# Cross-covariance attention and multiplicative FFN on one core: the head reordered, with k's squares moved off TensorE

## The chip, the core and the metric

One NeuronCore of a Trainium2 chip runs the whole kernel. The metric is device time in microseconds (us) of one launch. The engines are TensorE (PE, its weight loads PEld), VectorE (DVE), ScalarE (ACT), GpSimd (POOL) and SyncE (SP). SP, ACT and POOL also issue DMAs.

## What is computed

```python
# q, k, v: (4, 5824, 256) float32; tau = 1; B = 4, N = 5824, C = 256
qn = q / (norm(q, axis=1) + 1e-6)          # norms over the 5824 tokens, one for each channel
kn = k / (norm(k, axis=1) + 1e-6)
a  = softmax(kn.transpose(0, 2, 1) @ qn / tau)      # 256 x 256 for each batch
x  = (v @ a).reshape(23296, 256)
out = ((x @ w1) * (x @ w2)) @ w3 @ w_out            # w1, w2: 256 x 1024, w3: 1024 x 1024, w_out: 1024 x 256
```

## The kernel before

Everything is bf16 in SBUF and float32 in PSUM. v @ a @ w1 is taken as v @ (a @ w1): for each batch the 256 x 256 softmax is folded into w1 and w2, which gives `Wf`, 256 x 2 x 1024. Likewise w3 @ w_out becomes one matrix `W_sb`, 1024 x 256. So the main loop has, for each batch b, 12 chunks c of 512 tokens (the last of 192) and 8 columns j of 128: one **slot** is `emit_ab` (L621), with two matmuls for `a` and two for `b` at L627, a cast of `a` to bf16 on ScalarE (L633) and the product `abh` on VectorE (L644). Some slots later `abh` is multiplied by `W_sb` (`emit_half` L675 for the first chunks, `seven_products` L540 with POOL sums after those) and stored from SP. Batch 0 has 96 slots.

**The head**, before slot 0. q and k of batch 0 arrive in six pieces each (128 partitions x 8 rows x 256; the last has 5 rows and 64 left-over tokens), loaded and cast by DMAs that POOL issues (`load_piece`, `load_part`, L120; left-overs L117). The first half of piece 0 comes uncast through SP and ACT (`raw`, L745). TensorE works through the pieces in order: `squares` (L236) puts the 128 x 128 products of k with itself and of q with itself into PSUM, whose diagonals are the squared norms; `products` (L248) adds to `G`, the unnormalised scores. `busy` (L224) issues matmuls on zeros. After the last pieces come, all through `soft_units(0)`:

- `k_first` (L259): k's diagonal, on VectorE; `k_row` (L311): a float32 matmul with ones spreads it over all partitions; `k_step` (L319): Ln, Exp, Ln, Exp on ScalarE give 1/norm, `kr`.
- `q_first` (L328): q's diagonal; `scaled_first`: `scale` (L350) is G times `kr` for one half, `q_norm` (L339 to L342) Ln, Exp, add, reciprocal; then `exps` (L355) for two halves.
- `first_folds`: row sums (L375), the first 256 columns of the folds (`quarter_mm`, L422), their scaling (L431 ScalarE, L433 VectorE) into `Wf`. The next 256 columns and the second 512 (`second_quarter`, `fold`, L398) come in between the first slots.

**The order.** `make_agenda` lists for each batch what is emitted when, by a `clock` that counts the costs of what TensorE was given. For batch 0: three transposes of v on TensorE (L143, copies L145 on ScalarE or L147 on VectorE), the transposes of w3 and of v by DMA on SP (L757, L166), eight `w_unit`s (L837) that make `W_sb`, and the loads of the next batch's q and k, called (qk, 1, piece), and of v. Each load stands on POOL's queue behind `gate` (L615), a 1 x 1 copy from the newest `abh`; (qk, 1, 0) and (qk, 1, 2) stand behind a `hold` (L619) besides, a copy from `vT`, so that POOL's queue stops until SP's transpose of v piece 2 and of v piece 3 has landed.

**Scores of the next batch** run inside batch b's slots. `score_units` (L180) gives four units for each pair of rows, 92 in all: two with a square on ScalarE (L197) and two matmuls into G (L200), two with an add on VectorE (L212). In batch 0 they run from slot 36 to slot 78; `share` gives 32 of them (`EARLY`) to the slots ahead of slot 46 and the others evenly to the rest. A piece holds 16 units.

**The end.** `emit_out` (L687) with the last 192 columns of batch 3: `oleft` is copied by VectorE (L718) and stored for batches 2 and 3 by two DMAs of SP (L721); the last rows are copied by ScalarE (L723) and stored by a DMA of ACT (L725).

Of the kernel before, what the change touches and what calls it, by code (L numbers as in the profile page):

```python
# [25 lines left out]
def kernel(  # L26
# [198 lines left out]

    S = {}

    def squares(nm, pi, slots, end=False):

        if nm not in S:  # L230
            S[nm] = psum.tile([P, CT, P], F32, name=f"sq{nm}_0", **bank("out"))
        t = pieces[nm, 0, pi]
        for i in slots:
            for ct in range(CT):
                cs = slice(ct * P, (ct + 1) * P)
                nc.tensor.matmul(  # L236
                    S[nm][:, ct, :], lhsT=t[:, i, cs], rhs=t[:, i, cs],
                    start=(pi == 0 and i == 0 and ct == 0),
                    stop=(end and i == slots[-1] and ct == CT - 1), skip_group_check=True,
                )  # L240
# [13 lines left out]
    def soft_units(n):  # L254
        st = {}

        def k_first():
            d = work.tile([P, CT, P], F32, tag="sq", name="dk", bufs=2)
            nc.vector.tensor_mul(d, S["k"], ident.unsqueeze(1).to_broadcast([P, CT, P]))  # L259
            st["ksq"] = d.rearrange("p c t -> p (c t)")  # L260

        def scaled_first():
            scale(0)
            q_norm(st["ss"])
            scale(1)
            exps(0)
            exps(1)
# [40 lines left out]
        def k_row():  # L308

            m = psum.tile([P, 512], F32, name=f"row_{n}", **bank("ab"))  # L310
            nc.tensor.matmul(m[:, :C], lhsT=ones_pp, rhs=st["ksq"], start=True, stop=True)  # L311
            st["row"] = m[:, :C]
            st["kr"] = work.tile([P, C], F32, tag="kr", name=f"kr_{n}", bufs=1)
            for i in range(4):
                k_step(i)
# [99 lines left out]
        def quarter_mm(lo, c1, c2):  # L415

            if c2 == 0:
                tag = "ab" if lo == 0 else "out"
                st[lo, c1] = psum.tile([P, 2, 256], F32, name=f"quarter_{lo}_{c1}", **bank(tag))
            m = st[lo, c1]  # L420
            for w in range(2):
                nc.tensor.matmul(  # L422
                    m[:, w, :], lhsT=st["e"][:, c2, c1 * P : (c1 + 1) * P], rhs=w12[:, c2, w, lo : lo + 256],
                    start=(c2 == 0 and w == 0), stop=(c2 == CT - 1 and w == 1), skip_group_check=True,
                )
            if c2 == CT - 1:
                for o in (0, P) if lo == 0 else (slice(0, 256),):
                    cols = slice(o, o + P) if lo == 0 else o
                    dst, src = Wf[n][:, c1, :, lo : lo + 256][:, :, cols], m[:, :, cols]
                    if c1 == 0:  # L430
                        nc.scalar.activation(out=dst, in_=src, func=AF.Copy, scale=st["rs"][:, c1 : c1 + 1])  # L431
                    else:
                        nc.vector.tensor_scalar_mul(dst, src, st["rs"][:, c1 : c1 + 1])  # L433

        def first_folds():
            sum_mm(0)
            for c1 in range(CT):
                quarter_mm(0, c1, 0)
            sum_mm(1)
            for c1 in range(CT):  # L440
                quarter_mm(0, c1, 1)

        def second_quarter():
            for c1 in range(CT):
                for c2 in range(CT):
                    quarter_mm(256, c1, c2)

        if n == 0:
            return [k_first, k_row, q_first, scaled_first, first_folds, second_quarter, sum_start] + [lambda i=i: fold(i) for i in range(4, 8)]
# [28 lines left out]
    out_tiles = {}  # L478
    lefts = {}
# [207 lines left out]
    def emit_out(b, c, j, ab, only=None):  # L687
# [24 lines left out]
        if j == FT - 1:  # L712
            o = work.tile([P, 4, D], F32, tag="o_sb", name=f"osb_{b}_{c}", bufs=3)
            rows = out[b * N : b * N + NT * P, :].rearrange("(p i) c -> p i c", i=NT)
            if small:
                if b % 2 == 1 and only != 0:
                    o2 = work.tile([P, D], F32, tag="kr", name=f"oleft_{b}", bufs=1)
                    nc.vector.tensor_copy(o2, tl[1][:, 0, :])  # L718
                    for m in (b - 1, b):
                        k = (m - b + 1) * LEFT  # L720
                        nc.sync.dma_start(out=out[m * N + NT * P : (m + 1) * N, :], in_=o2[k : k + LEFT, :])  # L721
                if only != 1:
                    nc.scalar.copy(o[:, 0, :], tl[0][:, 0, :])  # L723
                    other = nc.scalar if b == B - 1 else nc.sync
                    other.dma_start(out=rows[:, NT - 1, :], in_=o[:, 0, :])  # L725
            else:
# [58 lines left out]
    load_piece("q", 0, 4, (half,))  # L785
    load_piece("k", 0, 5)
    soft0 = soft_units(0)
    whole = range(PIECE)
    lo, hi = range(half), range(half, PIECE)
    for sl in (lo, hi):  # L790
        squares("k", 0, sl)
        busy(2)
    for sl in (lo, hi):
        squares("q", 0, sl)
        products(0, sl)
    for pi in range(1, 4):
        squares("k", pi, whole)
        if pi < 3:
            busy(2)
        squares("q", pi, whole)  # L800
        products(pi, whole)
    load_piece("q", 0, 5, (1, 3, 4))
# [11 lines left out]
    for sl in (lo, hi):  # L814
        squares("q", 4, sl)
        products(4, sl)
    squares("k", 5, range(LAST + 1), end=True)
    soft0[0]()
    parts = [[LAST, 0], [1, 2], [3], [4]]
    for i, sl in enumerate(parts):  # L820
        end = i == len(parts) - 1
        squares("q", 5, sl, end=end)
        if end:
            soft0[2]()
        products(5, sl, end=end)
        if i == 0:
            soft0[1]()
# [19 lines left out]
    EARLY, EARLY_SLOT = 32, 46  # L847
# [18 lines left out]
    def make_agenda(b):  # L866
# [3 lines left out]
        if b == 0:  # L870
            at(0.5, 0.87, soft0[5])
            for i in range(4):
                at((1.7, 2.6, 3.5, 3.9)[i], 0.43, soft0[7 + i])
            at(4.6, 0.5, lambda: transpose_half_on_pe(0, 0, 1, False))
            at(7.0, 0.5, lambda: transpose_half_on_pe(0, 1, 0, True))
# [14 lines left out]
        for nm, m, pi, t in moves:  # L890
            if (nm, m, pi) in (("qk", 1, 0), ("qk", 1, 2)):
                at(t, 0.0, lambda i=2 + pi // 2: hold(vTs[0][0][:1, i * PIECE, 0, :1]))
# [87 lines left out]
```

## Time and profile before

| what | value |
|---|---|
| time, median of 3 runs | 557.34 us (557.31 to 557.48) |
| profiled execution: its own time | 557.51 us |
| its span, first to last instruction | 555.5 us |
| granted TensorE clock, mean | 0.998 |
| PE busy | 543.3 us, 98% of the span |
| DVE busy | 421.1 us, 76% |
| ACT busy | 366.7 us, 66% |
| POOL busy | 305.4 us, 55% |
| DMA | 77.60 MB, mean 140 GB/s |

Times in the profile count from the span's start. A timeline row has start, duration, engine, line, operation, tile written and tiles read, count, and in brackets the idle time of the engine ahead of it with what ended it. A row of the chain of waits has start, duration and what the end of the run hung on in that stretch. L-numbers are lines of the kernel.

### The profile page before, as it was taken

How to read it: one execution, taken by the hardware profiler on the slowest of the kernel's cores; microseconds unless marked ns; L12 is line 12 of the kernel's file. 1: busy time of each engine (PE TensorE's matmuls, PEld its weight loads, DVE VectorE, ACT ScalarE, POOL GpSimd, SP SyncE). 2: the span in 40 equal slices, each digit the busy share in tenths (PEclk: the TensorE clock that was granted, in tenths of full speed). 3: DMA queues.
4: the chain of work that ended last, by engine and by line, in shares of the span. 5: the costliest groups of instructions: out<-in, count | busy, mean ns of one | idle time of the engine just before them, and what ended most of it. 6: DMA issues, size and time to landing. Idle time of an engine off the chain costs nothing.

```text
span 555.5 us, 12406 instructions
## 1 busy us (share of the span) xinstructions
PE 543.3 (98%) x4697; PEld 355.7 (64%) x4697; DVE 421.1 (76%) x766; ACT 366.7 (66%) x740; POOL 305.4 (55%) x258
## 2 busy tenths in 40 slices
PE   7899999999999999999999999999999999999997
PEld 5764577666666666666667566666666666666665
DVE  2047748799976797888876688888877688888984
ACT  1046647688866877877766778787766566666663
POOL 4260020867789588898887588898977400010000
PEclk9999999999999999999999999999999999999999
DMA  9999988987566977675555767875651245343102
GB/s 212 211 182 209 159 153 199 219 181 136 127 147 153 181 148 163 134 159 131 121 127 133 153 133 167 174 142 118 153 114 39 81 110 125 87 112 84 77 39 95
DMA packets 75115, 77.60 MB, mean 140 GB/s; under 512 B 54192, under 2 KB 58800, under 8 KB 75056
## 3 DMA queue, kind: packets, MB, share of 16 engines
q0 software_dynamic: 15760, 38.93, 40.4%
q1 hardware_dynamic: 59008, 37.23, 24.0%
q8 instruction: 36, 0.59, 0.4%
q10 hardware_dynamic: 288, 0.66, 0.4%
q14 instruction: 23, 0.19, 0.1%
HBM read 78.91 MB, written 23.86 MB: 185 GB/s over the span
## 4 chain that ended last, share of the span: by engine, by line
PE 86%; DMA 9%; POOL 1%; ACT 1%; DVE 1%; issue 1%; POOLq 0%; ACTq 0%
PE a L627 27%; PE b L627 27%; PE prodA L540 12%; PE prodC L540 6%; PE G L200 5%; DMA k<-in_k_dram 4%; PE prodB L540 3%; DMA v<-in_v_dram 2%; PE fold L398 2%; DMA q<-in_q_dram 2%; PE o_out L706 2%; PE w L837 1%; DMA vT<-v 1%; POOL k L120 1%; POOL q L120 0%
## 5 line engine op out<-in xcount | busy, mean ns | idle before, releaser
L644 DVE TENSOR_TENSOR abh<-as,b 128x512 bf16<-128x512 bf16 x352 | 239.9, 684 | 85.1 <-ACT as L633 81.5
L633 ACT CAST as<-a 128x512 bf16<-128x512 f32 (+1 forms) x384 | 215.8, 563 | 93.3 <-PE a L627 63.4
L627 PE MATMUL a<-vT,Wf 128*128 128x512 bf16 x704 | 209.4, 379 | 0.4 <-ACT Wf L431 0.4
L627 PE MATMUL b<-vT,Wf 128*128 128x512 bf16 x704 | 209.4, 379 | 0.0
L627 PEld LDWEIGHTS <-Wf 128*128 128x128 bf16 x1536 | 141.4, 98 | 101.5 <-issue 0.8
L540 PEld LDWEIGHTS <-S 128*128 128x128 bf16 x1248 | 82.6, 98 | 34.3
L212 DVE TENSOR_TENSOR acc<-acc,sq 128x512 f32<-128x512 f32 x132 | 91.5, 693 | 2.7 <-ACT sq L197 1.9
L550 ACT COPY osb<-prodA 128x256 f32<-128x256 f32 x156 | 58.1, 373 | 42.7 <-PE prodA L540 42.2
L559 POOL TENSOR_TENSOR S<-abh,abh 128x1024 bf16<-128x1024 bf16 x29 | 61.8, 2131 | 31.5 <-DVE abh L644 16.4
L540 PEld LDWEIGHTS <-abh 128*128 128x128 bf16 x936 | 62.0, 98 | 25.7 <-issue 0.2
L562 POOL TENSOR_TENSOR S<-S,abh 128x1024 bf16<-128x1024 bf16 x29 | 61.7, 2128 | 1.9
L562 POOL TENSOR_TENSOR S<-abh 128x1024 bf16<-128x1024 bf16 x29 | 61.8, 2132 | 0.1
L562 POOL TENSOR_TENSOR S<-abh,S 128x1024 bf16<-128x1024 bf16 x29 | 61.8, 2133 | 0.1
L615 POOL COPY gate_t<-abh 1x1 bf16<-1x1 bf16 x39 | 7.3, 186 | 79.9 <-DVE abh L644 79.7
L200 PE MATMUL G<-k,q 128*128 128x256 bf16 x276 | 48.3, 273 | 0.9 <-DMA k<-in_k_dram 0.9
L540 PE MATMUL prodA<-comb_T,S 128*128 128x128 bf16 x624 | 47.6, 219 | 0.0
L197 ACT ACTIVATE sq<-q 128x512 f32<-128x512 bf16 x69 | 43.8, 634 | 0.0
L197 ACT ACTIVATE sq<-k 128x512 f32<-128x512 bf16 x69 | 43.5, 631 | 0.0
L553 DVE TENSOR_TENSOR osb<-prodC,osb 128x256 f32<-128x256 f32 x78 | 32.5, 417 | 0.0
L619 POOL COPY gate_t<-vT 1x1 bf16<-1x1 bf16 x2 | 0.4, 178 | 55.0 <-DVE abh L644 37.6
L200 PEld LDWEIGHTS <-q 128*128 128x128 bf16 x276 | 23.6, 98 | 4.2 <-issue 1.0
L540 PE MATMUL prodB<-W_sb,abh 128*128 128x128 bf16 x312 | 23.8, 219 | 0.1
(128 smaller groups left out, 449.6 us busy)
## 6 DMA issues: line engine op xcount, KB each, us to landing
out_dram<-osb SPq DMA_DIRECT2D x44, 512.0 KB, 3.4
k<-in_k_dram POOLq DMA_DIRECT2D x19, 512.0 KB, 8.7
v<-in_v_dram POOLq DMA_DIRECT2D x19, 512.0 KB, 5.7
q<-in_q_dram POOLq DMA_DIRECT2D x18, 512.0 KB, 5.8
w_wout<-in_moe_w_dram POOLq DMA_DIRECT2D x1, 2048.0 KB, 22.8
k<-in_k_dram POOLq DMA_DIRECT2D x4, 320.0 KB, 7.1
v<-in_v_dram POOLq DMA_DIRECT2D x4, 320.0 KB, 4.8
q<-in_q_dram POOLq DMA_DIRECT2D x3, 320.0 KB, 5.3
```

The source lines that it names most:

```text
L197: nc.scalar.activation(out=sqs[0][:, :, part, :], in_=src[:, o : o + 2, :], func=AF.Square)
L200: nc.tensor.matmul(G[:, ct, :], lhsT=qt[:, i, ct * P : (ct + 1) * P], rhs=kt[:, i, :], start=(pr == 0 and part == 0 and ct == 0), stop=(pr ...
L212: nc.vector.tensor_add(accs[n], accs[n], sqs[0][:, part - 2])
L398: nc.tensor.matmul(m, lhsT=st["e"][:, c2, c1 * P : (c1 + 1) * P], rhs=w12[:, c2, w, lo:hi], start=(c2 == 0), stop=(c2 == CT - 1),)
L540: nc.tensor.matmul(st[nm][:, i, :], lhsT=a[:, j, i * P : (i + 1) * P], rhs=w[j], start=(first and j == 0 and i == 0), stop=(j == 3), skip_ ...
L550: nc.scalar.copy(quarter(r, d), st["A"])
L553: nc.vector.tensor_add(quarter(r, d), st[nm], quarter(r, d))
L559: adder.tensor_add(x, a21, a22)
L562: adder.tensor_sub(x, u, w)
L627: nc.tensor.matmul(t[:, :n], lhsT=Wf[b][:, ct, w, j * P : (j + 1) * P], rhs=rhs_of(b, c, ct), start=(ct == 0), stop=(ct == CT - 1),)
L633: nc.scalar.copy(a_sb[:, :n], tiles[0][:, :n])
L644: nc.vector.tensor_mul(ab, a_sb, tiles[1])
```

## The change

- The squares of k pieces 0 to 3 leave TensorE. `add_k_squares` squares two rows at a time on ScalarE (16 instructions of 128 x 512); the first goes straight into the PSUM tile `kacc`, the others are added there by VectorE (15 adds). `squares` on TensorE does pieces 4 and 5 of k only.
- The four calls of `busy(2)` (8 matmuls on zeros, in pieces 0 to 2) give way to `busy_long(1)` after piece 0 and `busy_long(2)` after piece 2: float32 matmuls of ones, 512 wide.
- k's last piece is loaded ahead of the second half of q piece 4, which is cut into two loads of two rows.
- `k_early` adds up `kacc` and puts it through the ones matmul; `k_row` adds the diagonal of pieces 4 and 5 to the same PSUM row. k_row and its four ScalarE steps are issued ahead of q piece 5 instead of inside it.
- `scaled_first` does both `scale`s ahead of `q_norm`.
- `quarter_mm` becomes `narrow_fold`: columns 0 to 128, then 128 to 256, each with a PSUM tile of its own.
- One copy of a transposed v (piece 1, first half) goes from ScalarE to VectorE.
- `EARLY` goes from 32 to 28, and (qk, 1, 2) no longer stands behind a `hold`.
- The very last store (left-over rows of batch 3) goes from SP to ACT, behind ACT's own last store.

```diff
+    def busy_long(k):
+
+        m = psum.tile([P, 4, P], F32, name=f"warm_{nc.get_next_instruction_name()}", **bank("ab"))
+        for _ in range(k):
+            nc.tensor.matmul(
+                m, lhsT=ones_pp, rhs=ones_pp.unsqueeze(1).to_broadcast([P, 4, P]), start=True, stop=True,
+                skip_group_check=True,
+            )
+
+    kacc = []
+
+    def add_k_squares(pi):
+
+        for i in range(0, PIECE, 2):
+            src = pieces["k", 0, pi][:, i : i + 2, :]
+            if not kacc:
+                kacc.append(psum.tile([P, 2, C], F32, name="kacc", tag="out0", bufs=1))
+                nc.scalar.activation(out=kacc[0], in_=src, func=AF.Square)
+                continue
+            sq = work.tile([P, 2, C], F32, tag="sq", name=f"ksq_{pi}_{i}", bufs=2)
+            nc.scalar.activation(out=sq, in_=src, func=AF.Square)
+            nc.vector.tensor_add(kacc[0], kacc[0], sq)
...
+        def k_early():
+            kk = work.tile([P, C], F32, tag="kk", name="kk", bufs=1)
+            nc.vector.tensor_copy(kk, kacc[0][:, 0, :])
+            nc.vector.tensor_add(kk, kacc[0][:, 1, :], kk)
+            m = psum.tile([P, 512], F32, name=f"row_{n}", **bank("ab"))
+            nc.tensor.matmul(m[:, :C], lhsT=ones_pp, rhs=kk, start=True, stop=False, skip_group_check=True)
+            st["row"] = m[:, :C]
...
         def scaled_first():
-            scale(0)
+            for ct in range(CT):
+                scale(ct)
             q_norm(st["ss"])
-            scale(1)
             exps(0)
             exps(1)
...
-            m = psum.tile([P, 512], F32, name=f"row_{n}", **bank("ab"))
-            nc.tensor.matmul(m[:, :C], lhsT=ones_pp, rhs=st["ksq"], start=True, stop=True)
-            st["row"] = m[:, :C]
+            nc.tensor.matmul(
+                st["row"], lhsT=ones_pp, rhs=st["ksq"], start=False, stop=True, skip_group_check=True
+            )
...
-        def quarter_mm(lo, c1, c2):
+        def narrow_fold(lo, hi, c1, c2):
 
             if c2 == 0:
-                tag = "ab" if lo == 0 else "out"
-                st[lo, c1] = psum.tile([P, 2, 256], F32, name=f"quarter_{lo}_{c1}", **bank(tag))
+                tag = "ab" if lo < 256 else "out"
+                st[lo, c1] = psum.tile([P, 2, hi - lo], F32, name=f"narrow_{lo}_{c1}", **bank(tag))
...
         def first_folds():
-            sum_mm(0)
+            for c2 in range(CT):
+                sum_mm(c2)
+                for c1 in range(CT):
+                    narrow_fold(0, P, c1, c2)
             for c1 in range(CT):
-                quarter_mm(0, c1, 0)
-            sum_mm(1)
-            for c1 in range(CT):
-                quarter_mm(0, c1, 1)
+                for c2 in range(CT):
+                    narrow_fold(P, 2 * P, c1, c2)
...
+                        if m < B - 1:
+                            store()
+                        else:
+                            last_rows.append(store)
...
+                    if last_rows:
+                        last_rows.pop()(queue=nc.scalar)
...
     load_piece("k", 0, 4)
-    load_piece("q", 0, 4, (half,))
+    new_piece("q", 0, 4)
+    load_part("q", 0, 4, 0, half)
     load_piece("k", 0, 5)
+    load_part("q", 0, 4, half, half + 2)
+    load_part("q", 0, 4, half + 2, PIECE)
...
-    for sl in (lo, hi):
-        squares("k", 0, sl)
-        busy(2)
+    add_k_squares(0)
     for sl in (lo, hi):
         squares("q", 0, sl)
         products(0, sl)
+    busy_long(1)
     for pi in range(1, 4):
-        squares("k", pi, whole)
-        if pi < 3:
-            busy(2)
+        add_k_squares(pi)
         squares("q", pi, whole)
         products(pi, whole)
+        if pi == 2:
+            busy_long(2)
...
     squares("k", 4, whole)
-    for sl in (lo, hi):
+    squares("q", 4, lo)
+    products(4, lo)
+    soft0[7]()
+    squares("k", 5, range(LAST + 1), end=True)
+    soft0[0]()
+    for sl in (range(half, half + 2), range(half + 2, PIECE)):
         squares("q", 4, sl)
         products(4, sl)
-    squares("k", 5, range(LAST + 1), end=True)
-    soft0[0]()
-    parts = [[LAST, 0], [1, 2], [3], [4]]
-    for i, sl in enumerate(parts):
-        end = i == len(parts) - 1
-        squares("q", 5, sl, end=end)
-        if end:
-            soft0[2]()
-        products(5, sl, end=end)
-        if i == 0:
-            soft0[1]()
+    soft0[1]()
+    for sl in ([LAST, 0], [1, 2], [3]):
+        squares("q", 5, sl)
+        products(5, sl)
+    squares("q", 5, [4], end=True)
+    soft0[2]()
+    products(5, [4], end=True)
     soft0[3]()
...
-    EARLY, EARLY_SLOT = 32, 46
+    EARLY, EARLY_SLOT = 28, 46
...
-            at(7.0, 0.5, lambda: transpose_half_on_pe(0, 1, 0, True))
+            at(7.0, 0.5, lambda: transpose_half_on_pe(0, 1, 0, False))
...
-            if (nm, m, pi) in (("qk", 1, 0), ("qk", 1, 2)):
-                at(t, 0.0, lambda i=2 + pi // 2: hold(vTs[0][0][:1, i * PIECE, 0, :1]))
+            if (nm, m, pi) == ("qk", 1, 0):
+                at(t, 0.0, lambda: hold(vTs[0][0][:1, 2 * PIECE, 0, :1]))
```

## Prediction, on record before the change was run

> **What bounds the kernel now.** I read the page first (PE busy 98%), then PE's waits, then the chain of waits up to 60 us, then the timelines around the two places where PE waits, with POOL's queue beside them. From slot 36 to the end PE stands still once for any length; all other waits lie in the head. In the list of PE's waits (us in total, times, longest) after 60 us there is one line:
>
> ```profile
> PE G L200 <- DMA k<-in_k_dram: 0.9, 1, 0.9
> ```
>
> The head is bound by DMA: windows of 5 us from 5 to 30 us move 207 to 219 GB/s, and PE waits for q's pieces. The chain of waits shows what follows the last of them:
>
> ```profile
> 21.34 10.29 DMA q<-in_q_dram
> ...
> 32.40 0.45 PE row L311 x2
> ...
> 34.27 0.42 ACT kr L319
> ...
> 34.72 0.42 DVE s L350
> ...
> 35.45 0.52 ACT e L355
> ...
> 37.54 0.61 PE a L627 x2
> ```
>
> From 31.63, when q's last rows begin to land, to slot 0 at 37.54 is 5.9 us: PE's backlog with the row matmul in it, k's four ScalarE steps, the scaling, q's norm, exps, sums, the first fold. But a head that ends sooner helps only if the next thing is there sooner. PE's timeline at slot 36 and POOL's queue show the next thing, the first scores of batch 1:
>
> ```profile
> 82.58 1.04 PE L675 MATMUL o<-W_sb,abh 128*128 128x256 bf16 x8
> 83.45 0.60 PE L200 MATMUL G<-k,q 128*128 128x256 bf16 x4
> ```
>
> ```profile
> 75.01 0.18 POOL L619 COPY gate_t<-vT 1x1 bf16<-1x1 bf16 x1 [37.55 <-DVE abh L644]
> ...
> 76.30 0.55 POOL L120 DMA_DIRECT2D k<-in_k_dram  x1
> ...
> 96.06 0.18 POOL L619 COPY gate_t<-vT 1x1 bf16<-1x1 bf16 x1 [17.40 <-DMA vT<-v]
> ...
> 97.33 0.54 POOL L120 DMA_DIRECT2D k<-in_k_dram  x1
> ```
>
> ```profile
> 105.33 0.60 PE L200 MATMUL G<-k,q 128*128 128x256 bf16 x4 [0.85 <-DMA k<-in_k_dram]
> ```
>
> The load of k piece 0 of batch 1 is issued at 76.30 and lands 7.1 us later, at 83.4; PE comes to it at 83.45, just behind. The load of its piece 2, held until 96.06, is issued at 97.33, lands 8.0 later, and PE waits 0.85 for it.
>
> **What the skill says.** "TensorE: Matmul & The Clock Gate", Part 1: after an idle window of about 3.4 us the clock falls to half until PE has been busy as long. The trace agrees at the start (ten zero matmuls 0.43 apart up to 4.2, 0.22 later); its longest gap after that is 1.9 (16.95 to 18.81), with no slow matmul behind it. "SBUF — State Buffer", Who interferes with whom: a VectorE instruction with one SBUF input at most doesn't block GpSimd; the new adds read PSUM and one SBUF tile, so they should not hold up POOL's DMA issues. No row of before shows both at once. "DMA: Bandwidth & Descriptors", Queues, rings and completion order: each DMA engine takes turns between the queues that have work. This bears on the dropped hold: the transpose of v piece 2 landed 4.3 after its issue at 70.64 with nothing beside it, that at 121.04 took 6.8 beside loads.
>
> **The change, part by part.** Times are of the profiled execution, 557.51 (span 555.5 and 2.0 around it), 0.17 above the median of 557.34.
>
> *Squares of k off PE; fillers.* 64 square matmuls at 0.056 (16 take 0.89, 15.84 to 16.73) are 3.6 us, and 8 zero matmuls at 0.22 are 1.7. They end in waits for q (3.7 us in four), so taking them away gives nothing. Added: 16 ScalarE squares at 0.63 (row L197) and 15 adds at 0.69 (L212), 10 us each, on engines that do nothing between 10 and 30 us in the windows; k piece 3 lands at 21.0 (4.51 + 16.5), so kacc is complete by about 24.5 and k_early not late. The float32 fillers: two row matmuls of 256 take 0.45, so 0.9 each at 512 (0.4 to 1.8). After q piece 0 PE is free at 9.7 and q1 lands at 13.15; after q2, PE is free at 21.45 and q3 lands at 23.5, so two fillers end at 23.25: covered, with 0.25 to spare. The longest idle stretch becomes 15.8 (q1 done) to 18.8 (q2 lands), 3.0 us. Nearly 3.4; if the clock does fall, q2 is 1.5 us longer, of which 0.65 would still be there at the first `a`.
>
> *k ahead of q.* Bytes are the same, so q's last row still lands at 32.5 (27.51 + 5.0); k piece 5 lands near 28.9 instead of 30.25. PE then has k5's squares, the row matmul and k's four steps (1.83) done by 33.5, ahead of their use. The row matmul's 0.45 leaves PE's backlog behind 31.63, so q's diagonal is done at 34.03 instead of 34.48. Both scales now stand ahead of q_norm's add on VectorE: 34.03 plus about 0.75, so the add starts near 34.75 instead of 35.06. **0.3 gained** (0 to 0.45). The price is one DMA more: q's last piece, in five, took 2.05 us (30.45 to 32.5) for 320 KB where full ones (1.24 for 256 KB) would take 1.55, so a cut costs about **0.1** (0 to 0.2) of DMA time.
>
> *Narrow folds.* Between the sums of the two halves stand 4 fold matmuls of 128 columns instead of 256, 0.2 us less; e was ready at 36.36, the second sum ran at 36.52. **0.12 gained** (0 to 0.2). The next 128 columns, 8 x 0.056, lie in PE's wait for `Wf` (0.37). Scaling stays 128 wide on both engines.
>
> *Copy to VectorE.* ScalarE's copy took 1.01 and made the casts behind it late; PE's `b` at 49.23 came 0.2 late for an `abh`. VectorE has gaps of 0.4 to 1.1 there and takes 0.69. **0.2 gained** (0 to 0.2).
>
> So slot 0 comes 0.4 sooner and slot 10 about 0.6. **Where does it go?** Slot 32 (75.63) needs the transpose of v piece 2, landed at 74.95: room for 0.6. Slot 36's first unit needs k (1,0) at 83.4, and that hangs on no work of PE: POOL's hold waits for the same transpose, which waits on SP behind four transposes of w3, which wait for w3's load, landed at 59.3 at the end of the DMA stream that started at 1.2. The edits move none of these. PE arrives at 82.85 and waits 0.6: the head's gain is given back, and the DMA cut's 0.1 with it: **net +0.1** (-0.6 to +0.3).
>
> *hold and EARLY.* Without the hold the loads of (qk, 1, 2) follow the gate at clock 49, an `abh` of about 88.05, and land near 97 to 99 (v piece 3, ahead of them, lands at 91.65). With 28 units ahead of slot 46 and 2 a slot after, unit 32 comes at slot 48, near 109. **0.85 gained**; no later wait of PE stands ready to take it: k (1,3) had landed at 111.6 for slot 56, k (1,5) at 131.8 for slot 72 (144.6), and the loads after follow PE by their gates. The price: the transpose of v piece 3 (91.67 to 95.9) now runs beside loads, perhaps 3 us more, for slot 48 at 109: covered by 10 us. Four units more fall after slot 46: two adds (1.43), where VectorE was busy 37.25 of 40.4 us (109.6 to 150). The idle 3.1 should take them; **0.1** (0 to 1.4).
>
> *Last store.* SP's second store was issued at 552.24 and landed 2.3 later, the last; ACT's issue at 551.86 took 0.36, so behind it the next starts at about 552.24 too and lands after 2.3 to 2.5. VectorE, SP and the rest of the end are the same. **+0.05** (-0.1 to +0.2).
>
> Sum: 557.51 + 0.1 - 0.85 + 0.1 + 0.05 = 556.91, 0.6 less; from the median, **556.7**. What a measurement can tell from no change is about 0.2%, 1.1 us: this forecast lies inside it.
>
> **Rivals.** (1) *The head's gain is kept*, since the load of k (1,0) comes sooner with it. For: nothing but 15 us of DMA transposes, whose pace may differ, stands between w3 and it. Against: that chain has no PE in it. Then -0.6 more and no +0.1: 556.0, to 555.6 with the bounds. (2) *VectorE becomes the bound from slot 46 to 78*: its lag then holds back PSUM banks of `b`, and all of the 1.43 us counts. For: 98% busy in windows like 140 to 150. Against: PE lost nothing there, and ScalarE was what VectorE waited for (4.0 us from 105 to 155). It decides once VectorE's idle time there is used up; the 0.85 is more than eaten: 557.34 - 0.85 + 1.43 + 0.15 = 558.1, slower than before. (3) *The dropped hold doesn't do it*: POOL's queue is late for another reason and PE waits as long for k (1,2): 557.4.
>
> **Numbers.** Forecast 0.58 (556.3 to 557.1), rival 1 0.28, rival 2 0.09, rival 3 0.05. Range 555.6 to 557.7: it leaves out the far end of rival 1 and rival 2. Faster by over 0.2% (under 556.2): nearly all of rival 1 and a little of the forecast, 0.30. Slower by over 0.2% (over 558.45): half of rival 2 and an unforeseen stall in the head, 0.07. Within: 0.63.
>
> **What would show it.** In the changed profile: the first `a` near 37.1; `b` without a gap at slot 10; PE waiting about 0.6 for k at slot 36, near 83.5, which refutes rival 1; q and k of (1, 2) issued near 88 and no wait near 105; PE at 100% in 110 to 150 with VectorE at 96%, or gaps of PE behind `abh`, which is rival 2; matmuls 0.11 apart at 18.8 if the clock fell; the last landing within 0.2 of 2.9 us after VectorE's `oleft` copy. Wrong if slot 36 is reached without a wait, or if PE has waits after it that before did not have.

## The result, and the profile after

The changed kernel takes **563.11 us** (median of 15 runs, 557.37 to 566.62), the kernel before 557.79 beside it (15 runs, 556.81 to 558.71): ratio **1.0085 [1.006, 1.0109]**, slower. The forecast was 556.7, in a range that ended at 557.7. The profiled execution took 564.67 with a span of 562.9, 7.4 more than before; PE was busy 543.9 us (before 543.3), so nearly all of what came is idle time of PE. The changed kernel also scatters over 9 us where the kernel before scatters over 2. The ratios in this document are not those of the medians: they leave out runs that took over 1.5% more than the fastest of their kernel (1 of 15 here, 3 of 20 in e5, 1 of 4 in e13, 2 of 20 in e14), which in these kernels may simply be the longest stalls, so that the ratios rather understate the loss.

Read PE's waits first, as before. After 60 us, in the changed kernel (us in total, times, longest):

```profile
PE a L658 <- ACT as L664: 6.2, 1, 6.2
PE G L200 <- DMA k<-in_k_dram: 0.6, 2, 0.4
```

The wait of 0.9 for k has gone, and one of 6.2 for a cast of ScalarE has come. It is one place, slot 48. PE's timeline there:

```profile
108.12 0.60 PE L200 MATMUL G<-k,q 128*128 128x256 bf16 x4
114.88 1.01 PE L658 MATMUL a<-vT,Wf 128*128 128x512 bf16 x2 [6.15 <-ACT as L664]
...
117.39 0.83 PE L658 MATMUL a<-vT,Wf 128*128 128x512 bf16 x2
118.05 0.59 PE L658 MATMUL b<-vT,Wf 128*128 128x512 bf16 x2
```

Two things cost time here: the 6.15, and what follows it, since a pair of matmuls of one and the same shape takes 1.01 at 114.88 and 0.59 at 118.05. "ACT as" says only who came last. ScalarE's own timeline says why the cast was late: ahead of it in ScalarE's order stands a copy into an output buffer, which waited for a store to leave that buffer.

```profile
112.72 0.59 ACT L712 COPY osb<-o 128x512 f32<-128x512 f32 x1 [9.02 <-DMA out_dram<-osb]
...
114.25 1.06 ACT L664 CAST as<-a 128x512 bf16<-128x512 f32 x2
```

That store is the first that SP issues for batch 0. SP's queue in the changed kernel (start, duration of the issue):

```profile
91.19 7.23 SPq L166 DMA_TRANSPOSE vT<-v  x1
98.53 3.06 SPq L716 DMA_DIRECT2D out_dram<-osb  x3
```

The same queue in the kernel before:

```profile
91.67 1.90 SPq L166 DMA_TRANSPOSE vT<-v  x1
93.68 16.95 SPq L685 DMA_DIRECT2D out_dram<-osb  x4
```

The transpose of v piece 3 held SP for 7.2 us instead of 1.9, so the first store was issued 4.9 later; it then landed 14.1 after its issue (98.53 to 112.64) where it had taken 3.4 (93.68 to 97.07). From the DMA view (the last number is us from issue to landing), of the changed kernel:

```profile
vT<-v SPq DMA_TRANSPOSE x1, 18.9
```

The same line of the kernel before:

```profile
vT<-v SPq DMA_TRANSPOSE x1, 4.3
```

What ran beside it is in POOL's timeline of the changed kernel, the counterpart of the one shown of before:

```profile
88.85 0.53 POOL L120 DMA_DIRECT2D q<-in_q_dram  x1 [0.36 <-PE a L658]
89.37 0.54 POOL L120 DMA_DIRECT2D k<-in_k_dram  x1
...
95.10 0.58 POOL L120 DMA_DIRECT2D q<-in_q_dram  x1 [0.27 <-PE a L658]
110.66 0.53 POOL L120 DMA_DIRECT2D k<-in_k_dram  x1 [14.98 <-DMA vT<-v]
```

Without the hold, q and k of (1, 2) are issued ahead of the transpose (91.19) and q of (1, 3) in the middle of it; k of (1, 3) needs v piece 3's buffer and waits 15 us for the transpose itself. q's load of 95.10 landed at 110.07, with the transpose. SP was held by the transpose until 98.42, just before k of (1, 2), issued ahead of it, landed (98.67). The windows say that this is no sharing of a full pipe (after the busy times: PEclk, DMA share, GB/s). Changed kernel:

```profile
100.00:102.00 2.00, 2.00 (x17) 1.42 (x15) 1.97 (x4) 1.29 (x3) 0.00 (x0) 1.00 1.08 27
102.00:104.00 2.00, 2.00 (x17) 1.40 (x16) 1.97 (x4) 0.86 (x2) 0.00 (x0) 1.00 1.72 60
104.00:106.00 2.00, 2.00 (x17) 1.41 (x15) 1.05 (x2) 0.00 (x0) 0.00 (x0) 1.00 0.83 50
...
110.00:112.00 2.00, 0.00 (x0) 0.10 (x1) 0.00 (x0) 0.00 (x0) 1.32 (x2) 0.76 0.84 309
112.00:114.00 2.00, 0.00 (x0) 0.00 (x0) 0.00 (x0) 1.28 (x3) 2.00 (x4) 0.50 1.04 254
```

The same windows of the kernel before:

```profile
100.00:102.00 2.00, 2.00 (x17) 1.41 (x15) 2.00 (x4) 1.16 (x3) 1.99 (x5) 1.00 0.99 201
102.00:104.00 2.00, 2.00 (x17) 1.40 (x16) 1.97 (x4) 1.25 (x3) 2.00 (x3) 1.00 1.07 213
```

From 100 to 104, at a higher DMA share than before, the engines moved 27 and 60 GB/s instead of 201 and 213; from 104 to 106 it was 50 at a share of 0.83. The row of 112 to 114 shows the last cost: late in the stall PEclk is 0.50, and matmuls stay slow until about 117.8.

**The sum of the 7.4 us.** Slot 48 was at 109.67 before. Later k of (1, 0) puts 0.34 on it (first G at 83.79 instead of 83.45), the wait at 105 takes 0.85 off, two G units moved past slot 46 take 0.44 off: 108.72. The stall of 6.16 makes it 114.88, where the trace has it. From slot 48 to the end it is 448.0 instead of 445.8: the same 0.44, 0.2 for a later wait of G, and the rest, 1.6, the half clock (some 3 us of work, 114.88 to 117.8, at half speed are an estimate of 1.5). Together +7.4.

### The profile page after: what moved, and what is told of

Same layout as the page of the kernel before. It is cut to its first block, busy times and chain, and to the rows that moved or that the text cites. A ratio compares the mean times of both kernels' runs of the same rounds, so it can differ in the third digit from the quotient of the medians.

```text
span 562.9 us, 12336 instructions
## 1 busy us (share of the span) xinstructions
PE 543.9 (97%) x4634; PEld 354.4 (63%) x4641; DVE 433.1 (77%) x784; ACT 376.0 (67%) x755; POOL 306.0 (54%) x258
## 4 chain that ended last, share of the span: by engine, by line
PE 82%; DMA 12%; SPq 1%; POOL 1%; ACT 1%; issue 1%; DVE 1%; ACTq 0%; POOLq 0%
PE a L658 26%; PE b L658 26%; PE prodA L571 12%; PE prodC L571 6%; DMA k<-in_k_dram 5%; PE G L200 4%; PE prodB L571 3%; DMA out_dram<-osb 3%; DMA v<-in_v_dram 2%; PE fold L429 2%; DMA q<-in_q_dram 2%; PE o_out L737 2%; SPq L166 1%; PE w L879 1%; DMA w<-in_moe_w_dram 1%
## 5 line engine op out<-in xcount | busy, mean ns | idle before, releaser
L200 PE MATMUL G<-k,q 128*128 128x256 bf16 x276 | 47.0, 273 | 0.6 <-DMA k<-in_k_dram 0.6
L571 PE MATMUL prodA<-W_sb,abh 128*128 128x128 bf16 x312 | 24.2, 221 | 0.0
```

The source lines that it names most:

```text
L200: nc.tensor.matmul(G[:, ct, :], lhsT=qt[:, i, ct * P : (ct + 1) * P], rhs=kt[:, i, :], start=(pr == 0 and part == 0 and ct == 0), stop=(pr ...
L571: nc.tensor.matmul(st[nm][:, i, :], lhsT=a[:, j, i * P : (i + 1) * P], rhs=w[j], start=(first and j == 0 and i == 0), stop=(j == 3), skip_ ...
```

## The experiments

Ratios are to the kernel before, run beside each: its median was 557.66 beside e1 to e4, 557.90 beside e5 to e8, 557.45 beside e9 to e12 and 557.39 beside e13 to e15. "The transpose" is that of v piece 3, "the third load" is q of (1, 3), "the first store" is SP's first after the transpose.

### Which part of the change it is

**e1: the changed kernel with the hold back.**

```diff
-            if (nm, m, pi) == ("qk", 1, 0):
-                at(t, 0.0, lambda: hold(vTs[0][0][:1, 2 * PIECE, 0, :1]))
+            if (nm, m, pi) in (("qk", 1, 0), ("qk", 1, 2)):
+                at(t, 0.0, lambda i=2 + pi // 2: hold(vTs[0][0][:1, i * PIECE, 0, :1]))
```

> The changed kernel with the hold in front of (qk, 1, 2) put back, all else as changed. Theory (the dropped hold is the whole loss: loads beside the transpose of v piece 3 stretch it from 4 us to 19, and SP's stores behind it): the transpose takes 4 to 5 us again, no wait of 6 us near slot 48, EARLY 28 alone removes the wait of 0.85 near 105, and the head's gain is given back at slot 36: about 0.6 us under the kernel before, between -1.2 and 0. Rival (the head's edits, such as the clock that fell behind q piece 1, or the four units moved past slot 46, cost as well): 1 us or more above the kernel before.

556.59 (11 runs, 556.12 to 557.12), ratio 0.9981 [0.9972, 0.9989]. The transpose took 4.3 again, SP's issue of it 1.9, the first store landed at 96.42, and PE's only wait after 60 us is the one for k at slot 36:

```profile
PE G L200 <- DMA k<-in_k_dram: 0.4, 1, 0.4
```

So the dropped hold is needed for the loss. Is it enough?

**e2: the kernel before without that hold, and nothing else.** The edit is e1's, the other way round, on the kernel before.

> The kernel before with only the hold in front of (qk, 1, 2) dropped. Theory (the dropped hold): the transpose of v piece 3 takes 10 us or more, PE waits near slot 48, and the time is 3 to 8 us above the kernel before, as in the changed kernel. Rival (it takes the changed head too, or EARLY 28): within 1 us of the kernel before, the wait of 0.85 near 105 gone.

557.12 (14 runs, 556.07 to 558.81), ratio 0.9995 [0.9985, 1.0004]: no loss. The theory that the hold alone does it fell. But the trace has the stretch: transpose 13.0 (92.41 to 105.45), SP held for 6.05, first store landed at 106.30, and ScalarE's copy waited 1.9 for it (in the kernel before it waits 0.7 at this place for PE's own result, and nothing for a store); PE lost about 0.25 us. The stretch is there and falls short of what PE has in hand.

**e3: the kernel before with EARLY 28, and nothing else.**

```diff
-    EARLY, EARLY_SLOT = 32, 46
+    EARLY, EARLY_SLOT = 28, 46
```

> The kernel before with only EARLY 28 instead of 32. Theory: piece 2 is asked for at slot 48 instead of 46, some 3 us later, and k (1,2) has landed at 105.3 by then, so the wait of 0.85 goes although the hold stays: 0.5 to 0.9 us under the kernel before. Rival (VectorE is bound behind slot 46): the wait goes, but PE stands behind abh or b for as long, 0 to 0.6 us above.

556.66 (17 runs, 555.82 to 557.72), ratio 0.9981 [0.9973, 0.9989]. The wait at 105 is gone with the hold in place (span 554.5 against 555.5), and VectorE cost PE nothing: from 110 to 150 it was busy 38.16 of 40 us, PE all 40. The window (PE, PEld, DVE, ACT, POOL busy, PEclk, DMA share, GB/s):

```profile
110.00:150.00 40.00, 40.00 (x357) 26.74 (x356) 38.16 (x68) 34.89 (x69) 29.86 (x23) 1.00 0.73 152
```

The four units moved back are enough by themselves: k of (1, 2) still lands at 105.82, but PE comes to it only at 107.81. The hold didn't have to go.

**e4: the changed kernel with the hold back and EARLY at 32**, so the head, the copy and the last store alone.

```diff
-    EARLY, EARLY_SLOT = 28, 46
+    EARLY, EARLY_SLOT = 32, 46
```

> The changed kernel with the hold put back and EARLY 32 again: of the change only the head and the last store are left. Theory (the head's gain is given back at slot 36): PE comes to slot 36 some 0.4 us sooner and waits for k (1,0); PE waits again for k (1,2) near 105; within 0.4 us of the kernel before. Rival (the head's gain is kept): 0.5 to 0.8 us under it.

556.72 (13 runs, 556.12 to 557.52), ratio 0.9982 [0.9974, 0.999]. The theory that it would stay within 0.4 of the kernel before fell: it is 0.9 under. PE waited 0.2 at slot 36, and then had no wait at 105, since k of (1, 2) landed at 103.58 instead of 105.28: the chain of loads ahead of it had run about 0.9 faster. So the head's edits bring about 1 us too, but, as this trace has it, by clearing the same wait at 105 as EARLY does; e1, with both, has no more than either.

### Again, and in other company

**e5: the changed kernel once more**, with no edit.

> The changed kernel as it is, beside the next three on one chip. Theory (without the hold the transpose of v piece 3 runs beside loads and lasts 13 us or more; how much more decides whether PE waits): 2 to 6 us above the kernel before, and scattered by some us from run to run. Rival (the chip of the first measurement was the cause): within 1 us of the kernel before, as the kernel before without the hold was.

561.55 (20 runs, 556.46 to 567.54), ratio 1.0046 [1.0028, 1.0065]: slower again, scattered again. Its profiled execution (566.68, near the long end) repeats the pattern, longer: transpose 20.5, first store landed at 114.02, and in PE's waits:

```profile
PE a L658 <- ACT as L664: 7.6, 1, 7.6
```

**e6: the changed kernel with EARLY 32**, without the hold; the edit is e4's without e1's.

> The changed kernel without the hold, EARLY 32 again. If EARLY 28 (fewer squares and adds ahead of slot 46) is what makes the loss in the changed kernel, this is within 1 us of the kernel before; if it is the changed head (all DMAs shifted by one and PE early at slot 36), it is 2 to 6 us above, as the changed kernel.

557.17 (12 runs, 556.5 to 561.37), ratio 0.9993 [0.9975, 1.0011]. Transpose 13.9, third load issued at 95.58 (changed: 95.10), first store landed at 106.55; ScalarE waited 2.7 for it and PE 0.5.

**e7: the kernel before with EARLY 28 and without the hold.**

> The kernel before without the hold and with EARLY 28: the whole of the change except the head and the last store. If EARLY 28 without the hold is enough for the loss: 2 to 6 us above the kernel before. If the changed head is needed: within 1 us of it, no wait of PE near 105 and the transpose of v piece 3 at about 13 us.

560.84 (20 runs, 557.91 to 563.56), ratio 1.0049 [1.0031, 1.0067]. The loss is there without anything of the new head. Of the parts of the change it takes both: the dropped hold and EARLY 28. What EARLY 28 moves near there is the third load: it stands behind a gate of clock 56, which comes sooner when fewer G units lie ahead of it (issued at 95.14, in e2 at 96.16). In this profile (558.74, below its median) the transpose took 12.9 and the first store landed at 107.42.

### The transpose beside loads

**e8: the changed kernel with a hold on (qk, 1, 3) instead of (qk, 1, 2)**, so that only two loads run beside the transpose.

```diff
-            if (nm, m, pi) == ("qk", 1, 0):
-                at(t, 0.0, lambda: hold(vTs[0][0][:1, 2 * PIECE, 0, :1]))
+            if (nm, m, pi) in (("qk", 1, 0), ("qk", 1, 3)):
+                at(t, 0.0, lambda i=2 + pi // 3: hold(vTs[0][0][:1, i * PIECE, 0, :1]))
```

> The changed kernel with the hold in front of (qk, 1, 3) instead of (qk, 1, 2): only two loads, q and k of piece 2, may run beside the transpose, and the third, q of piece 3, not. If two loads are enough to stretch the transpose to 19 us: as slow as the changed kernel. If it is the third load, issued at 95.1 when the transpose's packets begin, that jams the queues: the transpose lands by about 101 and the time is 0 to 1 us under the kernel before.

556.85 (20 runs, 556.21 to 557.96), ratio 0.9979 [0.9971, 0.9986]. Transpose 9.2, first store landed at 102.64, ScalarE on time. Without the third load the loss is gone, and so is the wait at 105.

**e9: the changed kernel with four output buffers instead of three** (room for it: one buffer less for `e`, and `kk` in `kr`'s place).

```diff
-            st["o"] = work.tile([P, 4, D], F32, tag="o_sb", name=f"osb_{b}_{c}", bufs=3)
+            st["o"] = work.tile([P, 4, D], F32, tag="o_sb", name=f"osb_{b}_{c}", bufs=4)
```

> The changed kernel with four osb buffers instead of three (the room comes from one e buffer less and kk in kr's place). Theory (PE stands because ScalarE's copy into osb waits for the first store, which stands behind the transpose, and the casts of a stand behind that copy): ScalarE no longer waits near 104; what is left is the transpose itself, due at slot 48 near 108.4 and landing between 104 and 112: median 0 to 2 us above the kernel before, at least 2 us under the changed kernel, and PE's wait names vT instead of as. Rival (PE would have waited for the transpose as long anyway): as slow as the changed kernel.

556.56 (20 runs, 555.81 to 558.88), ratio 0.9991 [0.9983, 0.9998]: 5 us or more less than the changed kernel (563.11, in e5 561.55), and a little under the kernel before, where 0 to 2 us above it was expected. The transpose is as slow as ever (18.5) and the first store lands as late (111.93), but ScalarE's copy no longer waits for it, and of the 6.2 PE keeps 1.0, for the transposed rows themselves. ScalarE's timeline in e9:

```profile
104.17 0.58 ACT L712 COPY osb<-o 128x512 f32<-128x512 f32 x1 [0.72 <-PE o L706]
```

PE's timeline in e9:

```profile
109.48 0.61 PE L658 MATMUL a<-vT,Wf 128*128 128x512 bf16 x2 [1.00 <-DMA vT<-v]
```

This shows the path: store, its buffer, ScalarE's copy, the casts behind it, PE. It also gives the size of the cover that the prediction counted on: PE needs the transposed rows at 108.5, so the 18.5 us that the transpose took (90.89 to 109.43) used up all of it.

### How many loads, and when

**e10: the changed kernel with (qk, 1, 3) due at 57.5 instead of 56.**

```diff
-            moves = [("qk", 1, 0, 29.0), ("qk", 1, 1, 29.2), ("v", 0, 3, 33), ("qk", 1, 2, 49), ("qk", 1, 3, 56)]
+            moves = [("qk", 1, 0, 29.0), ("qk", 1, 1, 29.2), ("v", 0, 3, 33), ("qk", 1, 2, 49), ("qk", 1, 3, 57.5)]
```

> The changed kernel with the loads of (qk, 1, 3) due at clock 57.5 instead of 56, so that q of piece 3 is issued 1 to 2 us later than 95.1. If the moment of this third load is what EARLY 28 changes (95.0 to 95.1 where it jams, 95.6 to 96.2 where it doesn't): within 1 us of the kernel before, the transpose at 9 to 14 us. If it is something else in EARLY 28: 2 us or more above the kernel before, the transpose at 13 to 20 us.

556.71 (12 runs, 556.27 to 557.5), ratio 0.9991 [0.9982, 0.9999]. Third load issued at 96.69, transpose 12.1, first store landed at 104.07; ScalarE waited 0.8 for it, hardly more than its 0.7 for PE without a jam, and PE lost nothing.

**e15: e7 with the same due time**, 57.5.

> The kernel before without the hold, EARLY 28, third load due at clock 57.5: as in the run with the changed head, within 1 us of the kernel before if the moment of this load decides (the transpose at 9 to 13 us); 3 us above it if EARLY 28 without the hold is enough by itself.

557.59 (12 runs, 556.79 to 558.02), ratio 1.0005 [0.9996, 1.0013]: e7's loss is gone, with its EARLY 28 in place and its hold absent. Third load at 96.45, transpose 7.7. PE still waits 1.1 in this profile, since the first store landed only at 106.54.

**e11: e2 with (qk, 1, 3) due at 54.5**, to have the third load sooner with EARLY 32.

> The kernel before without the hold, EARLY 32, with the loads of (qk, 1, 3) due at clock 54.5 instead of 56, so that q of piece 3 is issued 1 to 2 us sooner than 96.2. If the moment of this load decides: 2 us or more above the kernel before, as with EARLY 28. If not: within 1 us of it.

556.51 (20 runs, 555.91 to 558.83), ratio 0.9989 [0.9981, 0.9997]. The edit moved the load by less than asked, to 95.25; transpose 11.0, first store 104.10, no loss. That is a miss for the theory that the moment alone decides: e7's third load, at 95.14, was only 0.1 sooner.

**e14: e7 with (qk, 1, 3) due at 54.5.**

> The kernel before without the hold, EARLY 28, third load due at clock 54.5. If the moment decides and sooner is worse: as slow as with 56 (3 us above the kernel before) or slower. If a certain meeting of the third load with the transpose's start decides, it may be fast: within 1 us.

558.73 (20 runs, 555.95 to 565.72), ratio 1.0016 [0.9998, 1.0034]: nearly 10 us of scatter. In its profile (563.07, far above its median) the third load was issued at 95.42, the transpose took 17.6 and PE lost 3.9. It settles nothing about the moment: e11's load came sooner and cost nothing.

**e13: e2 with (qk, 1, 3) due at 52**, so early that k of (1, 3) also goes ahead.

> The kernel before without the hold, EARLY 32, with the loads of (qk, 1, 3) due at clock 52 instead of 56: q of piece 3 is issued some 3 us sooner, ahead of the transpose's packets. If the moment of the third load alone decides: 2 us or more above the kernel before, transpose 15 us or more. If something else in EARLY 28 is needed: within 1 us of the kernel before.

583.38 (4 runs, 575.33 to 587.65), ratio **1.0422 [1.0346, 1.0497]**. q and k of (1, 3) were issued at 92.87 and 93.39: four loads beside the transpose, which took 34.0 and held SP for 17.3. So this run changes the number of loads as well as their moment, and can't be counted for the moment alone. PE's waits in e13:

```profile
PE b L627 <- DVE abh L644: 29.6, 1, 29.6
```

VectorE's timeline in e13:

```profile
125.80 0.69 DVE L644 TENSOR_TENSOR abh<-as,b 128x512 bf16<-128x512 bf16 x1 [31.72 <-DMA vT<-v]
```

The path is another one here: no store, but the transpose itself holds up `abh`, which shares its pool of buffers with the pieces of v (L112, L642). PE goes on at 126.54, before the first store lands at 126.78.

Its windows (PE, PEld, DVE, ACT, POOL busy, then PEclk, DMA share, GB/s):

```profile
96.00:104.00 8.00, 0.98 (x8) 0.54 (x6) 0.00 (x0) 2.11 (x4) 2.27 (x2) 0.72 1.37 52
104.00:112.00 8.00, 0.00 (x0) 0.00 (x0) 0.00 (x0) 0.00 (x0) 0.00 (x0) 0.50 1.18 46
112.00:120.00 8.00, 0.00 (x0) 0.00 (x0) 0.00 (x0) 0.00 (x0) 0.00 (x0) 0.50 1.31 94
```

With every compute engine at rest for most of 24 us, the DMA engines are busy all the time and move 46 to 94 GB/s. SP issued its first store only at 109.07, so no store is needed for the jam: it is there with the transpose and the loads.

**All of it in one table**, from the single profile of each kernel (us; the last column is what PE stood behind this chain, so the 0.85 for k in the kernel before is not in it; in e7 the profile names PE for ScalarE's wait, but it ends with the landing of the store as in the others):

| kernel | loads beside | third load issued | transpose took | first store landed | ScalarE waited for it | PE stood |
|---|---|---|---|---|---|---|
| before, e1, e3, e4, e12 | 0 | after it | 4.3 | 96.2 to 97.2 | 0 | 0 |
| e8 | 2 | after it | 9.2 | 102.64 | 0 | 0 |
| e10 | 3 | 96.69 | 12.1 | 104.07 | 0.8 | 0 |
| e11 | 3 | 95.25 | 11.0 | 104.10 | 0 | 0 |
| e2 | 3 | 96.16 | 13.0 | 106.30 | 1.9 | 0.25 |
| e15 | 3 | 96.45 | 7.7 | 106.54 | 3.5 | 1.1 |
| e6 | 3 | 95.58 | 13.9 | 106.55 | 2.7 | 0.5 |
| e7 | 3 | 95.14 | 12.9 | 107.42 | 3.8 | 1.4 |
| e14 | 3 | 95.42 | 17.6 | 110.72 | 6.8 | 3.9 |
| changed | 3 | 95.10 | 18.9 | 112.64 | 9.0 | 6.2 |
| e5 | 3 | 95.00 | 20.5 | 114.02 | 10.5 | 7.6 |
| e9 (four buffers) | 3 | 94.86 | 18.5 | 111.93 | 0 | 1.0 |
| e13 (other path) | 4 | 92.87 | 34.0 | 126.78 | | 29.6 |

e9 and e13 apart, what PE loses follows from when the first store lands: nothing up to about 104, 0.25 to 1.1 near 106.5, and then nearly 1 us for each. How long the transpose takes follows only roughly from the number of loads beside it, with a wide scatter at three.

**Ahead or behind.** The traces hold more transposes of v than this one, and they show what the number of loads leaves out. 28 of them had one to four loads in flight that were all issued 0.6 us or more *behind* the transpose: these took 3.1 to 7.3 us and held SP for 1.2 to 3.2. In two the first load was issued within 0.6 us of the transpose; they took 9.2 and 9.4. The 12 with two loads issued 1.6 to 3.2 us *ahead* (the rows of the table with two loads or more) took 7.7 to 34.0 and held SP for 5.65 to 17.3; in all of them but e13, SP came free 0.1 to 0.3 us before k of (1, 2), the second of the two, landed. This was found in the traces afterwards: no run issued this transpose ahead of these loads.

### One step further

**e12: e1 with batch 1's scores from slot 37 instead of 36**, to be rid of the wait for k.

```diff
-    SLOTS0, SLOTS = (36, 78), (4, 71)
+    SLOTS0, SLOTS = (37, 78), (4, 71)
```

> The changed kernel with the hold put back and the scores of batch 1 begun at slot 37 instead of 36. Theory (the head's gain is given back at slot 36, where PE waits 0.4 for k (1,0)): PE comes to its first score matmul after k has landed and keeps the 0.4: 0.2 to 0.5 us under the kernel with the hold alone, 1.3 to 1.6 under the kernel before. Rival (the same units in fewer slots make VectorE late, or PE waits elsewhere): no faster than with the hold alone.

556.25 (21 runs, 555.76 to 557.61), ratio 0.998 [0.9973, 0.9986]. The wait at slot 36 went, and one of 0.4 came at slot 32, at 75.80. The profile puts it down to ScalarE's last copy into `W_sb`; the transpose of v piece 2, which slot 32 needs as well, landed at 75.75. e1, e3, e4, e8 and e12 all beat the kernel before by 0.2% (about 1.1 us), and their intervals don't tell them apart.

## Why the prediction was wrong, step by step

**The step that failed** is the price of the dropped hold: "the transpose of v piece 3 (91.67 to 95.9) now runs beside loads, perhaps 3 us more, for slot 48 at 109: covered by 10 us". Three things in it were wrong.
- *Size.* Not 3 us more but 5 to 16 more with two or three loads (9.2 to 20.5 in all, 7.7 once where the third load was hardly beside it). The 3 came from one row of before, a transpose that took 6.8 "beside loads". Its four loads stand 1.0 to 2.6 us behind it; those of the changed kernel stand 1.8 and 2.3 ahead. SP's queue and POOL's in the kernel before:

```profile
121.04 2.01 SPq L166 DMA_TRANSPOSE vT<-v  x1
```

```profile
122.06 0.55 POOL L117 DMA_DIRECT2D q<-in_q_dram  x1
...
123.67 0.58 POOL L120 DMA_DIRECT2D k<-in_k_dram  x1
```

  So the row was one of another case. (The row that it is set against, at 70.64, had no loads beside it, but two transposes of w3, which landed at 71.20 and 72.80.)
- *Who waits.* The cover was counted for the transpose's reader at slot 48. Behind the transpose on SP stands the first store, behind that (by its buffer) ScalarE's copy, behind that in ScalarE's order the casts, and PE behind them. In the kernel before, the store landed at 97.07 and the copy ran at 104.51, after a wait for PE's own result: this cover was 7.4 us, where slot 48 had 13 (95.94 to 109), and the store was late both by SP's longer hold (4.9) and by its own slow landing (10.7). Naming what stands behind the moved instruction on SP would have shown it. e9 shows this path.
- *What follows a stall.* It left PEclk at half: 1.6 more. The Trainium skill, "TensorE: Matmul & The Clock Gate", Part 1, gives about 3.4 us of idleness for that; here it came sooner. PE's last matmul ended at 108.72, and a PEclk of 0.76 in the window from 110 to 112 puts the fall near 111.0, after 2.3 us (0.50 in the windows from 112 to 116).

The prediction drew on the skill's "DMA: Bandwidth & Descriptors", Queues, rings and completion order, for engines taking turns between queues. Taking turns alone would divide the rate and not lower it; the trace has it falling from about 200 to 27 to 60 GB/s, so the measurement decides, and turns alone don't explain the jam.

**The rest, by its steps.**
- *Squares and fillers: nothing on the path.* Right in the time, not in the detail. PE did lose the clock (PEclk 0.64 from 18 to 21), after gaps of 2.5 and 2.1 us instead of the 3.0 foreseen, and the fillers ended at 24.02, 0.23 after q3 landed. The end of the head felt none of it: e4, whose clock stayed at 1.00, has its exps at 35.29, the changed kernel at 35.18. POOL's issues of DMAs beside the new adds took 0.53 to 0.56, as before.
- *k ahead of q: 0.3.* The exps came at 35.18 instead of 35.45, but that 0.27 is no gain: the 8 traces with the old head have their exps at 34.95 to 35.45 (mean 35.25), the 9 with the new one at 35.08 to 35.37 (mean 35.23). The kernel before was profiled at the late end. Not confirmed, and the cause is open; q's last row landed as forecast (mean 32.36 instead of 32.50).
- *Narrow folds: 0.12, first `a` near 37.1.* From the exps to the first `a` it was 2.08 or 2.09 in every trace of the old head. In the changed profile it was 2.32, by a term that wasn't priced, a load of w that the fold needs (before, it landed at 35.13):

```profile
35.18 0.91 ACT L386 ACTIVATE e<-s,r 128x256 bf16<-128x256 f32 x2 [0.51 <-DVE r L373]
...
36.31 0.33 PE L453 MATMUL narrow<-w,e 128*128 128x128 bf16 x3 [0.29 <-DMA w<-in_moe_w_dram]
...
37.50 0.60 PE L658 MATMUL a<-vT,Wf 128*128 128x512 bf16 x2
```

  In e1, e4, e10 and e12 this load landed in time, and the stretch was 1.99 or 2.00: a gain of 0.09, nearly as forecast. In the other five it was 2.16 to 2.40. So over all traces slot 0 came at 37.34 with the old head and at 37.40 with the new one (means): of the 0.4 that was forecast nothing is left.
- *Copy to VectorE.* The late `b` at 49.23 is gone, and slot 10 is gapless. From slot 0 to slot 10 all traces of the new head take 12.79 to 12.84, those of the old one 12.98 or more. Right.
- *Slot 36 takes the head's gain back.* Right in that PE waited for k, and its first G is a little later than before, not sooner. k of (1, 0) landed at 83.01 to 84.14 with the old head and at 83.33 to 84.95 with the new one. Rival 1 is out.

```profile
83.79 0.60 PE L200 MATMUL G<-k,q 128*128 128x256 bf16 x4 [0.41 <-DMA k<-in_k_dram]
```

  What the step did not see is that the head also moves the landing of k of (1, 2), worth 0.85 by itself (e4): with the hold in place it is 103.58 to 104.75 in the three traces of the new head and 105.28 and 105.82 in the two of the old.
- *hold and EARLY: 0.85.* The wait did go, and the loads were issued at 88.85 and 89.37 as foreseen (88). But EARLY alone is enough (e3); the hold was dropped for nothing and caused the loss together with EARLY's earlier gate (e7 against e2). They were costed in one sum, as if only their gains met.
- *VectorE from slot 46: 0.1, rival 2 1.43.* e3 has four units more there and PE loses nothing. Rival 2 is out; so is rival 3.
- *Last store: 0.05.* From SP's store of the left-over rows at 559.10 to the last landing it is 2.85 us (561.95); before, 2.85 from 551.70 (554.55). Worth nothing. SP at the end of the changed kernel:

```profile
559.10 0.49 SPq L752 DMA_DIRECT2D out_dram<-oleft  x1
```

ScalarE's queue there:

```profile
559.27 0.37 ACTq L762 DMA_DIRECT2D out_dram<-osb  x1
559.68 0.67 ACTq L752 DMA_DIRECT2D out_dram<-oleft  x1
```

Without the failed step the sum would have come near: 556.7 was forecast, and e1, which is the change without it, takes 556.59. That it comes so near is partly luck: e1 is 1.07 under the kernel before beside it (0.6 to 1.6 by its interval) where the forecast was 0.6, which started from a median of 557.34 and not 557.66.

**What stays open.** Why three loads beside one transpose give 8 us in one kernel and 20 in the next: the moment of the third load explains part of it (e10, e15), but not e11 against e14. Counted from the third load's issue to the moment when SP comes free of the transpose, the traces do fall into groups: 0.4 to 2.9 us in the six with 7.7 to 13.9 us, 3.3 to 3.7 in the four with 17.6 to 20.5 (98.42 less 95.10 is 3.3 in the changed kernel), 16.1 in e13. That was seen afterwards, in one profile of each, and no run tested it. Open too is what in the DMA engines makes the jam. Of loads issued by another engine or right behind the transpose, or a transpose cut in pieces, nothing was tried.

## What to carry to other kernels

A wait that keeps loads off a DMA transpose can be worth far more than it seems to cost: before removing it, write down everything queued behind that transpose, on its issuing queue, on the buffers of the stores there, and on the engines that reuse those buffers, and take the smallest cover. A price for it must come from a row where the loads stand on the same side of the transpose, ahead or behind. Where two edits aim at the same wait, try each alone; here moving four units of work gave the whole gain, and the second edit gave only its risk. And look at the scatter: here 9 us instead of 2 was the sign that the kernel had come to hang on a race between transfers. By the same token one profile of each kernel can't show a gain of 0.3 us.

## What the runs showed of the hardware

- **A DMA transpose and plain loads hurt each other, above all when the loads are ahead**: 4.3 us alone, 9.2 with two loads of 512 KB issued ahead of it, 7.7 to 20.5 with a third behind it, 34.0 with two more; 3.1 to 7.3 with all loads 0.6 us or more behind it. Load packets of 4 KB that take 0.32 us took up to 3.6 in the changed kernel from 102 to 104, and a packet of 8 KB on an instruction queue took 4.4 from 100 to 102 (0.32 in the kernel before).
- **A transpose behind loads holds its issuing queue**: SP was held by that one instruction for 1.9 us with nothing beside it, 5.65 to 7.6 with two loads ahead (0.1 to 0.3 short of their last landing, 11 traces), 17.3 with four.
- **The clock can fall after a gap of 2.5 us, and not always at once**: with the same head, PEclk fell to 0.64 in 12 to 15 us in e1, right behind a gap of 2.6. In the changed kernel it stayed up behind the same gap (2.5) and fell in 18 to 21, behind a second one of 2.1. It stayed at 1.00 in e4, where the gaps were 0.7 and 2.2. The skill's page on TensorE (Part 1) says that the window is free-running, so that it varies between runs of one kernel; that agrees.
- **Where an instruction fetch falls goes with when a load lands**: a packet of 16 KB on an instruction queue takes 0.89 to 0.98 us among plain loads. In the kernels with the old head it falls at 83.4 to 85.4, and q of (1, 1) lands 3.0 to 3.5 after k of (1, 0); with the new head it falls at 90.0 to 91.8, and q lands 2.5 after. All 17 traces agree. This may be where e4's 0.9 us came from; no edit tested it.
